# Second weight staged whole in the doubled filter's idle space, loads in one queue by need, four wide scaling products on GpSimd

## The chip, the cores and the metric

One core of a Trainium2 chip runs the kernel. The metric is the device time of one execution in microseconds (us). Every run named here was fast (granted TensorE clock 0.990 to 1.0 over the whole span; the granted clock is the share of full speed that the chip allows TensorE). Profiles come from one execution each; the span in a profile is some 2 us shorter than the time of its run.

## The reference, cut to what matters

```python
X = np.fft.rfft(x, axis=1)                 # x: (8, 3008, 256)
Y = X * (filt_r + 1j * filt_i)[None]       # a filter for each frequency and channel
x = np.fft.irfft(Y, n=3008, axis=1).reshape(24064, 256)
h = x @ w_in                               # 256 -> 2048
out = (h * sigmoid(beta * h)) @ w_out      # 2048 -> 256, float32
```

The kernel does each transform as two stages of small matmuls with a transposition between them (3008 = 47 x 64). Batch 0 is transposed on chip. From batch 1 on the transposition goes through DRAM: the first stage's result `a` is written to a scratch tensor `d` (the trace writes this "d<-a") and read back turned ("a<-d"). The feed-forward part runs all the while, and the transform of the next batch is slipped between its matmuls. An eviction is the copy of a matmul's result out of its accumulator into a tile.

## The kernel before: the parts that matter

The filter lives in two tiles. `fri` holds the real and the imaginary half; batch 0 uses it, so it is loaded first. `frr` holds the real half twice; only batch 1 and later need it, so for the first 46 us nothing is in it. The second weight must be scaled by 1/beta on its way to bf16. In the code `gp` and `nc.gpsimd` are GpSimd, `nc.sync` is SyncE, `nc.scalar` ScalarE; `place` slips work into the feed-forward loop.

```python
fri = consts.tile([P, NK, D], F32, ...)       # NK = 24 frequency groups, 3 MB
frr = consts.tile([P, NK, D], F32, ...)       # 3 MB, idle until batch 1
FG = ((0, KG), (KG, KG), (2 * KG, 2 * KG))    # parts of 6, 6 and 12 groups

def load_wout(f0, n):                         # a staging tile from a pool of two
    ws = ostp.tile([P, n, D], F32, name="ws", tag="ost")
    nc.sync.dma_start(ws[:], moe_w_out[f0 * P : (f0 + n) * P, :].rearrange(...))
    return ws

def scale_wout(ws, f0, n, eng):               # 4 calls x 4 products of 128x256
    for i in range(n):
        eng.tensor_scalar_mul(wout_sb[:, f0 + i, :], ws[:, i, :], rbeta_sb[:, f0 + i : f0 + i + 1])
# ... (first stage of batch 0, tables, loads of the first weight and of x1) ...
ws = [load_wout(i * WG, WG) for i in range(2)]
# ... (batch 0: products with fri, back transform) ...
for i in range(4):
    if i >= 2:
        ws.append(load_wout(i * WG, WG))      # waits for a staging tile, in SyncE's queue
    scale_wout(ws[i], i * WG, WG, gp)
for k0, n in FG:                              # the doubled filter: first part on SyncE, rest on GpSimd
    for at in (0, M):
        for go in load_filter(frr, filt_r, at, k0, n, gp if k0 else nc.sync):
            go()
# ... (feed-forward loop; slipped into it for batch 1:)
def s1(b, i, on_act):                         # first stage, then a write to DRAM
    ...
    if jj + 2 == JG:
        nc.sync.dma_start(s["d1r"][:, g * JG : (g + 1) * JG, :], s["a1"][:])      # d<-a, four per batch
def a2_read(b):                               # read back turned: a<-d, waits for all four writes
    for h in range(NG):
        nc.sync.dma_start(t[:], s["d1c"][:, h * KG : (h + 1) * KG, :])
```

In the trace of before, SyncE's transfers leave in program order: the third and fourth weight load wait 26.7 us in all for their staging tiles, and the filter's loads behind them leave only then, the first one at 46.27 us, right after the fourth weight load at 45.85.

Of the kernel before, what the change touches and what calls it, by code (L numbers as in the profile page):

```python
# [9 lines left out]
P = 128  # L10

ACT = mybir.ActivationFunctionType
ALU = mybir.AluOpType
F32 = mybir.dt.float32
BF16 = mybir.dt.bfloat16
# [9 lines left out]
M = 64  # L25
H = M // 2
NK = 24
J = 32
KG = 6
NG = NK // KG  # L30
JG = 8
# [5 lines left out]
def kernel(  # L37
# [10 lines left out]
    nc = tc.nc  # L48

    B, S, D = x.shape  # L50
    NF = filt_r.shape[0]
    DIN, FF = moe_w_in.shape
# [4 lines left out]
    NFB = FF // P  # L57
    NP = 2 * N1
# [7 lines left out]
    dpool = ctx.enter_context(tc.tile_pool(name="dram_scratch", bufs=2, space=bass.MemoryType.DRAM))  # L66

    def pool(name, bufs, **kw):
        return ctx.enter_context(tc.tile_pool(name=name, bufs=bufs, **kw))
# [3 lines left out]
    xpool = pool("xpool", 1)  # L73
# [6 lines left out]
    ostp = pool("ostp", 2)  # L80
# [5 lines left out]
    fri = consts.tile([P, NK, D], F32, name="fri", tag="fri")  # L86
    frr = consts.tile([P, NK, D], F32, name="frr", tag="frr")
# [9 lines left out]
    rbeta_sb = consts.tile([P, NFB], F32, name="rbeta_sb", tag="rbeta_sb")  # L97
    win_sb = wpool.tile([P, NDC, FF], BF16, name="win_sb", tag="win_sb")
    wout_sb = wpool.tile([P, NFB, D], BF16, name="wout_sb", tag="wout_sb")
# [3 lines left out]
    def evac(dst, src, on_act, scale=None):  # L103
        if on_act:
            nc.scalar.activation(dst, src, ACT.Copy, scale=1.0 if scale is None else scale)  # L105
        elif scale is None:
            nc.vector.tensor_copy(dst, src)  # L107
        else:
            nc.vector.tensor_scalar_mul(dst, src, scale)  # L109

    def load_x(b, parts):
        t = xpool.tile([NP, J, D], BF16, name="xg", tag="xg")
        xv = x[b].rearrange("(p j) d -> p j d", j=J)
        for p0, p1, j0, j1 in parts:
            nc.gpsimd.dma_start(t[p0:p1, j0:j1, :], xv[p0:p1, j0:j1, :])  # L115
        return t
# [3 lines left out]
    X_HALVES = [(0, 80, 0, J // 2), (80, NP, 0, J // 2), (0, 80, J // 2, J), (80, NP, J // 2, J)]  # L120
# [3 lines left out]
    def load_filter(f_sb, filt, at, k0, n, eng):  # L124
        lo = AP(filt.tensor, filt.offset + k0 * D, [[N1 * D, H], [1, n * D]])
        hi = AP(filt.tensor, filt.offset + (N1 - k0) * D, [[N1 * D, H], [-D, n], [1, D]])
        return [
            lambda: eng.dma_start(
                f_sb[at : at + H, k0 : k0 + n, :].rearrange("p k d -> p (k d)"), lo
            ),  # L130
            lambda: eng.dma_start(f_sb[at + H : at + M, k0 : k0 + n, :], hi),
        ]

    def load_wout(f0, n):
        ws = ostp.tile([P, n, D], F32, name="ws", tag="ost")
        nc.sync.dma_start(
            ws[:], moe_w_out[f0 * P : (f0 + n) * P, :].rearrange("(fb fp) j -> fp fb j", fp=P)
        )
        return ws

    def scale_wout(ws, f0, n, eng):
        for i in range(n):
            eng.tensor_scalar_mul(
                wout_sb[:, f0 + i, :], ws[:, i, :], rbeta_sb[:, f0 + i : f0 + i + 1]
            )


    sp = ctx.enter_context(ExitStack())
# [26 lines left out]
    def warm(n, cols=512):  # L175
        for _ in range(n):
            nc.tensor.matmul(pw[0][:, :cols], lhsT=wz[:, :P], rhs=wz[:, :cols], start=True, stop=True)
# [12 lines left out]
    gp = nc.gpsimd  # L190
# [6 lines left out]
    FG = ((0, KG), (KG, KG), (2 * KG, 2 * KG))  # L197
# [67 lines left out]
    def t2_part(h, part):  # L265
        u, r = us[h], rs[h]
        ks_ = slice(h * NH, (h + 1) * NH)
        if part == 0:
            nc.scalar.activation(t2[:, ks_, 2, :], u[:], ACT.Sin, scale=TWO_PI)
        elif part == 1:  # L270
            nc.scalar.activation(r[:], u[:], ACT.Abs)
        else:
            for cols, sgn, b in ((slice(0, H), -1.0, hp), (slice(H, M), 1.0, hm)):
                nc.scalar.activation(
                    t2[:, ks_, 1, cols], r[:, :, cols], ACT.Sin, scale=sgn * TWO_PI, bias=b[:]
                )

    def t2_more(h, eng):
        ks_ = slice(h * NH, (h + 1) * NH)
        eng.tensor_scalar_mul(t2[:, ks_, 4, :], t2[:, ks_, 1, :], -1.0)  # L280
        eng.tensor_copy(t2[:, ks_, 3, :], t2[:, ks_, 2, :])
        eng.tensor_copy(t2[:, ks_, 0, :], t2[:, ks_, 1, :])
# [10 lines left out]
    angles(0, nc.vector)  # L293
    angles(1, gp)

    for go in load_filter(fri, filt_i, M, *FG[2], gp):
        go()

    id_f = setup.tile([NFB, NFB], F32, name="id_f", tag="id_f")
    gp.tensor_copy(id_f[:], ident[:NFB, :NFB])  # L300
    tiny = setup.tile([NFB, P], F32, name="tiny", tag="tiny")
# [8 lines left out]
    held = setup.tile([P, 1], F32, name="held", tag="held")  # L310
    for p0 in (H, M + H):
        gp.tensor_copy(held[p0 : p0 + H], fri[p0 : p0 + H, 2 * KG - 1, :1])
    WI = 2
    for h in range(WI):
        fs = slice(h * FF // WI, (h + 1) * FF // WI)
        gp.dma_start(win_sb[:, :, fs], moe_w_in[:, fs].rearrange("(dc p) f -> p dc f", p=P))
    mark2 = dpool.tile([1, 2 * D], F32, name="mark2", tag="mark2")
    for c, p0 in enumerate((M - 1, P - 1)):
        nc.sync.dma_start(mark2[:, c * D : (c + 1) * D], fri[p0 : p0 + 1, 2 * KG - 1, :])
    WG = NFB // 4  # L320
    ws = [load_wout(i * WG, WG) for i in range(2)]


    a_t = ypool.tile([P, NDC, NK, J, 4], BF16, name="a_t", tag="y")

    def first1(i, on_act):
        for dc in range(NDC):
            if dc:
                ps = opsum.tile([P, 4, P], F32, name="psa", tag="acc")
            else:  # L330
                ps = fpsum.tile([P, 4, P], F32, name="psa", tag="f")
            for e in range(4):
                nc.tensor.matmul(
                    ps[:, e, :KP],
                    lhsT=x_cur[:, 4 * i + e, dc * P : (dc + 1) * P],
                    rhs=t1b[:],
                    start=True,
                    stop=True,
                )
            evac(  # L340
                a_t[:, dc, :, 4 * i : 4 * i + 4, :].rearrange("p k j a -> p j k a"),
                ps[:, :, :KP].rearrange("p j (k a) -> p j k a", a=4),
                on_act[dc],
            )
# [6 lines left out]
    warm(2)  # L351
    for part in (1, 2):
        t2_part(0, part)
    for i in range(3, 5):
        first1(i, (False, False))
        warm(2)
# [3 lines left out]
    first1(6, (True, True))  # L360
    warm(2)
    first1(7, (False, True))

    xs = {}
    if B > 1:
        xs[1] = load_x(1, X_HALVES)



    def table3(i, part, on_act):  # L370
        pt = opsum.tile([P, KG, P], BF16, name="pt", tag="acc")
        for e in range(KG):
            nc.tensor.transpose(
                pt[:, e, :],
                t2[:, KG * i + e, part : part + 2, :].rearrange("p c k -> p (c k)"),
                ident[:],
            )
        dst = t3 if part else t3b
        if i == 0:
            if part:  # L380
                evac(dst[:, 0, :], pt[:, 0, :], on_act, 0.5)
            else:
                nc.vector.tensor_scalar_mul(dst[:, 0, :], pt[:, 0, :], keep[:])
            evac(dst[:, 1:KG, :], pt[:, 1:KG, :], on_act)
        else:
            evac(dst[:, KG * i : KG * i + KG, :], pt[:], on_act)
# [76 lines left out]
    for i in range(NK // 2 + FLAG):  # L463
        if i < NK // 2:
            product(i)
        if i % 3 < 2 and i // 3 < 3:
            turn_a(2 + 2 * (i // 3) + i % 3, True)
        if i < 3:
            t2_part(1, i)
        if i % 3 > 0 and i // 3 < 3:  # L470
            table3(1 + i // 3, 4 - 2 * (i % 3), i % 3 == 1)
        if i == 3:
            t2_more(1, nc.vector)

            bps = hpsum.tile([P, NFB], F32, name="bps", tag="hps")
            nc.tensor.transpose(bps[:], bt[:], id_f[:])
            nc.vector.tensor_copy(beta_sb[:], bps[:])
            nc.vector.reciprocal(rbeta_sb[:], beta_sb[:])
        if i == 9:
            table4()  # L480
        if i >= FLAG:
            inverse3(i - FLAG)

    for i in range(4):
        if i >= 2:
            ws.append(load_wout(i * WG, WG))
        scale_wout(ws[i], i * WG, WG, gp)
    for k0, n in FG:
        for at in (0, M):
            for go in load_filter(frr, filt_r, at, k0, n, gp if k0 else nc.sync):  # L490
                go()

    ys = {}
# [218 lines left out]
    if B > 1:  # L712
        at = place(1, 11, u1(1, True), per=2)
        place(at + 1, at + 1, [lambda: a2_read(1)], per=9)
        at = place(22, 54, u23(1), per=2)
# [3 lines left out]
    if B > 2:  # L719
        place(36, 36, ux(2), per=9)  # L720
        at = place(50, 66, u1(2, True), per=3)
# [40 lines left out]
    for s in range(len(steps) + LAG):  # L762
        if s < len(steps):
            i, fb = steps[s]
# [4 lines left out]
            while pos < t0 + tn:  # L769
                b, n0 = divmod(pos, S)  # L770
# [18 lines left out]
        if s >= LAG:  # L789
            i, fb = steps[s - LAG]  # L790
# [18 lines left out]
            if fb == NFB - 1:  # L809
                ost = ostp.tile([P, 4, D], F32, name="ost", tag="ost")  # L810
                for h in range((nch + 1) // 2):
                    n = min(2, nch - 2 * h)
# [38 lines left out]
```

## Time and profile before

Before the change the median was 799.36 us (798.99 to 801.47, four runs).

| Reading | Value | View |
|---|---|---|
| TensorE busy | 772.4 of 797.2 us | page, busy line |
| TensorE waits for the read-back of batch 1 | 4.6 us, ends 71.2 us | waits, timeline |
| TensorE waits for an eviction whose buffer a d<-a write holds | 1.8 us, near 53 us | waits |
| last d<-a write, issue to landing | 8.6 us | chain |
| DMA share at 40 to 45 and 45 to 50 us | 0.42, 0.62 | table of stretches |

The page's busy line (us, share of the span, instructions):

```profile
PE 772.4 (97%) x6001; PEld 547.9 (69%) x6097; DVE 393.1 (49%) x642; ACT 597.2 (75%) x919; POOL 153.9 (19%) x161
```

TensorE's list of waits from 45 to 80 us (line, what it waited for: us in total, times, longest):

```profile
PE ps L611 <- DMA a<-d: 4.6, 1, 4.6
PE ps L512 <- ACT a L105: 1.8, 1, 1.8
```

SyncE's timeline (start us, us from the start of the first to the end of the last, queue, what, count). L136 is the fourth load of the second weight; L128 is the first of four loads of the doubled filter; L594 are the four d<-a writes; L601 is the read-back:

```profile
45.85 0.37 SPq L136 DMA_DIRECT2D ws<-in_moe_w_out_dram  x1
46.27 0.49 SPq L128 DMA_DIRECT2D frr<-in_filt_r_dram  x1
...
48.27 8.65 SPq L594 DMA_DIRECT2D d<-a  x4
65.40 1.77 SPq L601 DMA_DIRECT2D a<-d  x4
```

GpSimd's timeline: the last four scaling products, then the first of its eight loads of the doubled filter:

```profile
50.25 3.62 POOL L143 TENSOR_SCALAR wout_sb<-ws,rbeta_sb 128x256 bf16<-128x256 f32 x4 [0.84 <-DMA ws<-in_moe_w_out_dram]
53.82 0.56 POOL L128 DMA_DIRECT2D frr<-in_filt_r_dram  x1
```

The chain of waits from 44 to 72 us (start, us, what):

```profile
48.27 6.20 DMA d<-a
...
56.62 8.63 DMA d<-a
65.40 5.72 DMA a<-d
```

The table of stretches (the stretch, its length in us; then for TensorE, its weight loads, VectorE, ScalarE and GpSimd busy us and instruction count; then granted clock, DMA share, GB/s):

```profile
40.00:45.00 5.00, 4.95 (x40) 3.30 (x40) 3.69 (x6) 3.75 (x7) 2.80 (x4) 1.00 0.42 124
45.00:50.00 5.00, 5.00 (x37) 3.25 (x36) 2.55 (x4) 4.47 (x9) 4.41 (x5) 1.00 0.62 163
...
65.00:70.00 5.00, 1.57 (x11) 0.88 (x9) 0.42 (x1) 1.83 (x3) 0.00 (x0) 1.00 0.99 229
70.00:75.00 5.00, 3.61 (x20) 2.41 (x21) 2.62 (x4) 0.69 (x1) 1.03 (x1) 0.66 0.72 263
```

Read together: the fourth weight load leaves SyncE at 45.85 us, because it had to wait for a staging tile. The filter's first loads and the d<-a writes stand behind it. The last write is issued at 56.6 us and takes 8.63 us, the read-back another 5.72. TensorE has nothing to do from 66.6 to 71.2 us, and afterwards it gets a clock of 0.66 on average from 70 to 75 us. All the rest of the program is about 99% TensorE work (99.0 to 99.3 us in each 100 us from 200 to 700 us), so a microsecond that these waits lose is hardly made up later.

### The profile page before, as it was taken

What the parts mean: (1) busy time and instruction counts of PE and PEld (TensorE: products, weight loads), DVE (VectorE), ACT (ScalarE), POOL (GpSimd) and SP (SyncE); (2) the same over time, 40 slices, a digit from 0 to 9 for tenths busy, and PEclk for the clock granted to TensorE, in tenths of its full rate; (3) what the DMA queues carried; (4) which work ended last, traced back from release to release, by engine and by line L of the source; (5) the groups of instructions that cost most, each with busy time, mean ns of one, the idle gap of its engine ahead of it and who ended that gap; (6) DMA issues with size and microseconds to landing.
All of it is one profiled execution on the core that took longest, in us unless ns stands there. A gap on an engine that the chain in (4) does not pass through costs nothing.

```text
span 797.2 us, 15283 instructions
## 1 busy us (share of the span) xinstructions
PE 772.4 (97%) x6001; PEld 547.9 (69%) x6097; DVE 393.1 (49%) x642; ACT 597.2 (75%) x919; POOL 153.9 (19%) x161
## 2 busy tenths in 40 slices
PE   8897999999999999999999999999999999999997
PEld 5665767776677667776678766787667776776665
DVE  7834935674537556274644656357462770500100
ACT  6774887787678866788667886778767788677776
POOL 9371510340004300142001310023100340000000
PEclk9999999999999999999999999999999999999999
DMA  8987568324731168111780128602370114010101
GB/s 185 229 210 193 115 179 185 125 90 142 168 133 48 67 184 196 62 48 67 199 216 28 67 82 204 177 28 93 107 224 27 67 74 126 28 53 27 55 27 53
DMA packets 83733, 91.43 MB, mean 115 GB/s; under 512 B 3727, under 2 KB 74018, under 8 KB 82768
## 3 DMA queue, kind: packets, MB, share of 16 engines
q1 hardware_dynamic: 80446, 72.90, 29.4%
q0 software_dynamic: 2944, 17.30, 11.4%
q8 instruction: 47, 0.77, 0.4%
q10 hardware_dynamic: 272, 0.26, 0.1%
q14 instruction: 24, 0.20, 0.1%
HBM read 57.16 MB, written 46.66 MB: 130 GB/s over the span
## 4 chain that ended last, share of the span: by engine, by line
PE 87%; DMA 6%; DVE 3%; issue 2%; POOL 2%; ACT 0%; DVEq 0%; SPq 0%; ACTq 0%; POOLq 0%
PE acc L801 40%; PE hps L773 36%; DMA d<-a 3%; PE ps L589 3%; PE ps L512 3%; PE ps L611 2%; PE ps L637 2%; DMA fri<-in_filt_i_dram 1%; DMA a<-d 1%; DVE ost L107 1%; POOL xg L115 0%; DVE qb_t L432 0%; POOL r L260 0%; DVE pb_t L432 0%; DVE p_t L622 0%
## 5 line engine op out<-in xcount | busy, mean ns | idle before, releaser
L782 ACT ACTIVATE gT<-hps,beta_sb 128x512 bf16<-128x512 f32 x752 | 516.4, 687 | 181.9 <-PE hps L773 148.4
L801 PE MATMUL acc<-wout_sb,gT 128*128 128x256 bf16 x3008 | 455.8, 273 | 3.7 <-ACT ost L105 0.2
L773 PE MATMUL hps<-y,win_sb 128*128 128x512 bf16 (+7 forms) x1634 | 427.6, 350 | 0.4 <-DVE y L109 0.3
L801 PEld LDWEIGHTS <-gT 128*128 128x128 bf16 x3008 | 285.8, 98 | 132.4 <-issue 4.0
L773 PEld LDWEIGHTS <-win_sb 128*128 128x128 bf16 x1728 | 164.9, 98 | 24.9 <-issue 0.7
L627 POOL TENSOR_TENSOR v_t<-p_t,q_t 128x512 bf16<-128x512 f32 x84 | 106.7, 1270 | 370.6 <-DVE q_t L626 361.9
L107 DVE COPY ost<-acc 128x512 f32<-128x512 f32 x87 | 56.1, 683 | 195.3 <-PE acc L801 189.1
L107 DVE CAST a<-ps 96x512 bf16<-96x512 f32 x96 | 65.8, 687 | 89.1 <-PE ps L589 84.1
L109 DVE TENSOR_SCALAR y<-ps 128x376 bf16<-128x376 f32 (+2 forms) x120 | 64.5, 541 | 61.2 <-PE ps L512 61.0
L622 DVE TENSOR_TENSOR p_t<-ps,frr 128x512 f32<-128x512 f32 x84 | 58.1, 691 | 38.3 <-PE ps L611 36.9
L626 DVE TENSOR_TENSOR q_t<-ps,fri 64x512 f32<-64x512 f32 x84 | 58.3, 694 | 1.2
L623 DVE SCALAR_TENSOR_TENSOR q_t<-ps,fri 64x512 f32<-64x512 f32 x84 | 57.5, 684 | 1.1
L512 PEld LDWEIGHTS <-zz 96*128 96x128 bf16 x512 | 35.5, 98 | 31.4 <-issue 2.7
L105 ACT ACTIVATE z<-ps 128x512 bf16<-128x512 f32 x84 | 49.5, 589 | 0.4
L589 PE MATMUL ps<-xg,t 94*96 94x512 bf16 x112 | 41.9, 381 | 0.6
L512 PE MATMUL ps<-t,zz 96*128 96x94 bf16 x448 | 36.7, 204 | 1.1
L611 PE MATMUL ps<-a,t 128*128 128x256 bf16 x168 | 32.3, 274 | 5.6 <-DMA a<-d 5.3
L115 POOL DMA_DIRECT2D xg<-in_x_dram x22 | 12.0, 554 | 116.4 <-PE acc L801 97.7
L637 PE MATMUL ps<-v_t,t 128*128 128x256 bf16 x168 | 32.1, 273 | 0.3 <-DVE q_t L626 0.3
L611 PEld LDWEIGHTS <-t 128*128 128x128 bf16 x168 | 15.9, 98 | 20.1 <-issue 5.6
L589 PEld LDWEIGHTS <-t 94*96 94x96 bf16 x112 | 13.8, 123 | 11.9
L637 PEld LDWEIGHTS <-t 128*128 128x128 bf16 x168 | 15.6, 98 | 7.8 <-DVE q_t L626 0.5
(119 smaller groups left out, 201.9 us busy)
## 6 DMA issues: line engine op xcount, KB each, us to landing
out_dram<-ost SPq DMA_DIRECT2D x40, 512.0 KB, 2.8
d<-a SPq DMA_DIRECT2D x28, 384.0 KB, 7.0
a<-d SPq DMA_DIRECT2D x28, 384.0 KB, 5.6
d<-z SPq DMA_DIRECT2D x28, 384.0 KB, 2.3
zz<-d SPq DMA_DIRECT2D x28, 384.0 KB, 5.4
xg<-in_x_dram POOLq DMA_DIRECT2D x6, 1280.0 KB, 10.3
out_dram<-ost SPq DMA_DIRECT2D x20, 128.0 KB, 2.3
ws<-in_moe_w_out_dram SPq DMA_DIRECT2D x4, 512.0 KB, 23.9
```

The costliest lines, as they stand in the source:

```text
L107: nc.vector.tensor_copy(dst, src)
L109: nc.vector.tensor_scalar_mul(dst, src, scale)
L512: nc.tensor.matmul(ps[:, e, :NP], lhsT=zz[:, jj + e, dc * P : (dc + 1) * P], rhs=tab[:], start=True, stop=True,)
L589: nc.tensor.matmul(ps[:KP], lhsT=t1[:], rhs=s["x"][:, 2 * i : 2 * i + 2, :], start=True, stop=True)
L611: nc.tensor.matmul(ps[:, e, :], lhsT=t2[:, k0 + e, 3:5, :].rearrange("p c k -> p (c k)"), rhs=s["a2"][g][:, kk + e, :], start=True, stop=True,
L622: nc.vector.tensor_tensor(p_t[:], ps[:], frr[:, ks_, :], ALU.mult)
L626: nc.vector.tensor_tensor(q_t[:M], ps[M:P], fri[M:P, ks_, :], ALU.mult)
L627: nc.gpsimd.tensor_tensor(v_t[:], p_t[:], q_t[:], ALU.add)
L637: nc.tensor.matmul(ps[:, e, :], lhsT=t3[:, k0 + e, :], rhs=v_t[:, e, :], start=True, stop=True)
L773: nc.tensor.matmul(hps[:, pos - t0 : pos - t0 + ln], lhsT=win_sb[:, dc, fb * P : (fb + 1) * P], rhs=ys[b][:, dc, n0 : n0 + ln], start=(dc ...
L782: nc.scalar.activation(gT[:, :tn], hps[:, :tn], ACT.Silu, scale=beta_sb[:, fb : fb + 1])
L801: nc.tensor.matmul(acc[tb // 2][:, tb % 2, :], lhsT=gT[:, tb * P : (tb + 1) * P], rhs=wout_sb[:, fb, :], start=(fb == 0 and tb % 2 == 0), ...
```

## The change

The intent is to get rid of the wait for a staging tile. The weight goes in one piece into 16 of the 24 groups of `frr`, which is idle then. All its loads stand in GpSimd's queue, interleaved with x1 in the order of need; SyncE loads the free third of `frr` after a marker that waits for x1. The 16 products become four with a broadcast operand. Two small moves come with it: the last imaginary part of `fri` is issued from ScalarE, earlier than it was from GpSimd, and one eviction of a table goes from VectorE to ScalarE. Not in the cut below: x1's loads move up in the program, and SyncE's old marker before the weight loads (`mark2`, which waited for the second filter part) is gone. The core of the diff:

```diff
-    def load_wout(f0, n):
-        ws = ostp.tile([P, n, D], F32, name="ws", tag="ost")
-        nc.sync.dma_start(ws[:], moe_w_out[...])
+    def staged(i):
+        return frr[:, NK - NFB + i * WG : NK - NFB + (i + 1) * WG, :]
+    def load_wout(i):
+        nc.gpsimd.dma_start(staged(i), moe_w_out[i * WG * P : (i + 1) * WG * P, :].rearrange(...))
-        for i in range(n):
-            eng.tensor_scalar_mul(wout_sb[:, f0 + i, :], ws[:, i, :], rbeta_sb[:, f0 + i : f0 + i + 1])
+        nc.gpsimd.tensor_tensor(wout_sb[:, fs, :], staged(i),
+            rbeta_sb[:, fs].unsqueeze(2).broadcast_to([P, WG, D]), ALU.mult)
...
-    for go in load_filter(fri, filt_i, M, *FG[2], gp):          # after GpSimd's angle table
-        go()
+    for go in load_filter(fri, filt_i, M, *FG[2], nc.scalar):   # after ScalarE's first tables
+        go()
...
+    load_win(0); load_win(1); load_wout(0)
+    xs[1] = load_x(1, X_HALVES[:2])
+    load_wout(1)
+    load_x(1, X_HALVES[2:], xs[1])
+    nc.sync.dma_start(mark3[:], xs[1][:1, J - 1, :])            # holds SyncE until x1 is there
+    load_wout(2); load_wout(3)
...
-            table3(1 + i // 3, 4 - 2 * (i % 3), i % 3 == 1)
+            table3(1 + i // 3, 4 - 2 * (i % 3), i % 3 == 1 or i == 8)
...
-    for k0, n in FG:
+    for k0 in range(0, NK, JG):                                 # thirds of 8 groups
         for at in (0, M):
-            for go in load_filter(frr, filt_r, at, k0, n, gp if k0 else nc.sync):
+            for go in load_filter(frr, filt_r, at, k0, JG, gp if k0 else nc.sync):
                 go()
```

More of the change, by code (lines that the diff above doesn't have):

```diff
@@ L109, in evac, with load_x @@
             nc.vector.tensor_scalar_mul(dst, src, scale)
-    def load_x(b, parts):
-        t = xpool.tile([NP, J, D], BF16, name="xg", tag="xg")
+    def load_x(b, parts, t=None):
+        if t is None:
+            t = xpool.tile([NP, J, D], BF16, name="xg", tag="xg")
         xv = x[b].rearrange("(p j) d -> p j d", j=J)
@@ L132, in load_filter, with scale_wout @@
         ]
-    def load_wout(f0, n):
-        ws = ostp.tile([P, n, D], F32, name="ws", tag="ost")
-        nc.sync.dma_start(
-            ws[:], moe_w_out[f0 * P : (f0 + n) * P, :].rearrange("(fb fp) j -> fp fb j", fp=P)
-        )
-        return ws
-    def scale_wout(ws, f0, n, eng):
-        for i in range(n):
-            eng.tensor_scalar_mul(
-                wout_sb[:, f0 + i, :], ws[:, i, :], rbeta_sb[:, f0 + i : f0 + i + 1]
-            )
+    WG = NFB // 4
+    def staged(i):
+        return frr[:, NK - NFB + i * WG : NK - NFB + (i + 1) * WG, :]
+    def load_wout(i):
+        nc.gpsimd.dma_start(
+            staged(i),
+            moe_w_out[i * WG * P : (i + 1) * WG * P, :].rearrange("(fb fp) j -> fp fb j", fp=P),
+        )
+    def scale_wout(i):
+        fs = slice(i * WG, (i + 1) * WG)
+        nc.gpsimd.tensor_tensor(
+            wout_sb[:, fs, :],
+            staged(i),
+            rbeta_sb[:, fs].unsqueeze(2).broadcast_to([P, WG, D]),
+            ALU.mult,
+        )
     sp = ctx.enter_context(ExitStack())
@@ L312, with load_win @@
         gp.tensor_copy(held[p0 : p0 + H], fri[p0 : p0 + H, 2 * KG - 1, :1])
-    WI = 2
-    for h in range(WI):
-        fs = slice(h * FF // WI, (h + 1) * FF // WI)
+    def load_win(h):
+        fs = slice(h * FF // 2, (h + 1) * FF // 2)
         gp.dma_start(win_sb[:, :, fs], moe_w_in[:, fs].rearrange("(dc p) f -> p dc f", p=P))
-    mark2 = dpool.tile([1, 2 * D], F32, name="mark2", tag="mark2")
-    for c, p0 in enumerate((M - 1, P - 1)):
-        nc.sync.dma_start(mark2[:, c * D : (c + 1) * D], fri[p0 : p0 + 1, 2 * KG - 1, :])
-    WG = NFB // 4
-    ws = [load_wout(i * WG, WG) for i in range(2)]
+    load_win(0)
+    load_win(1)
+    load_wout(0)
+    xs = {}
+    if B > 1:
+        xs[1] = load_x(1, X_HALVES[:2])
+    load_wout(1)
+    if B > 1:
+        load_x(1, X_HALVES[2:], xs[1])
+        mark3 = dpool.tile([1, D], BF16, name="mark3", tag="mark3")
+        nc.sync.dma_start(mark3[:], xs[1][:1, J - 1, :])
+    load_wout(2)
+    load_wout(3)
     a_t = ypool.tile([P, NDC, NK, J, 4], BF16, name="a_t", tag="y")
@@ L362 @@
     first1(7, (False, True))
-    xs = {}
-    if B > 1:
-        xs[1] = load_x(1, X_HALVES)
     def table3(i, part, on_act):
@@ L484 @@
     for i in range(4):
-        if i >= 2:
-            ws.append(load_wout(i * WG, WG))
-        scale_wout(ws[i], i * WG, WG, gp)
-    for k0, n in FG:
+        scale_wout(i)
+    for k0 in range(0, NK, JG):
         for at in (0, M):
-            for go in load_filter(frr, filt_r, at, k0, n, gp if k0 else nc.sync):
+            for go in load_filter(frr, filt_r, at, k0, JG, gp if k0 else nc.sync):
                 go()
```

## The prediction

A gain of about 4.5 us off 799.35 gives 794.8. 250 to 270 GB/s for saturated DMA are an estimate from the table of stretches of before, where stretches with a share of 1.0 or more moved 191 to 282 GB/s (276, 282 and 261 from 50 to 65 us).

> **What bounds the kernel now.** TensorE: in the busy line of the profile it works 772.4 of 797.2 us (97%), and from 145 us on about 99% of every stretch in the table of stretches. The change touches only the first 75 us, so only TensorE's idle time there can be won. The list of its waits has two pieces that matter here:
> - 4.6 us at 66.6 us, for the read-back of batch 1's transposed first stage ("a<-d"). After it the granted clock is 0.66 from 70 to 75 us, and slow matmuls (four output matmuls in 0.85 us, not 0.44) cost about 1.3 us more. [...]
> - 1.8 us at 53.4 us, for an eviction that waited for the first "d<-a" write to free a buffer.
>
> Both come from SyncE's DMA queue. The third and fourth loads of the second weight (ws) wait there for a staging buffer; the fourth goes out at 46 us. Four filter loads follow, so the first d<-a issue comes at 48.3 us and the last at 56.6; that lands at 65.3, and its read-back gives data at 71.2 us. Meanwhile DMA's share is 0.42 at 40 to 45 us and 0.62 at 45 to 50, against 1.0 to 1.1 around it.
>
> **What the change does.**
> 1. All weight loads queue with x1 without waiting. The 40 to 50 us hole (about 1.1 MB below the saturated 250 to 270 GB/s, worth about 4 us) fills. SyncE's marker holds it until x1 has landed, at 42 to 43 us: the bytes up to there are the same and DMA is full from 5 to 40 us. First d<-a issue: about 45 us. The 1.8 us wait goes.
> 2. The scaling on GpSimd, 16 x 0.92 = 14.8 us, becomes four products of 128x1024. From v_t (1.27 us for 512) and u (1.46 us for 768) I estimate 2.0 to 2.5 us each. Off the critical path; it only sets when the filter's later two thirds load, from 50 to 53 us instead of 53.8.
> 3. The imaginary filter's last part goes out from ScalarE at about 12 us, not from GpSimd at 16.3. VectorE waited 1.2 us for it before the seventh product (27.7 us). But it now competes with the first part, and its two issues occupy ScalarE: I credit 0.3 us.
> 4. One table eviction (0.55 us) leaves VectorE, which is back to back from 27.7 to 35.4 us, for ScalarE: 0.4 us.
>
> **How much is critical.** The matmuls after the read-back start when the DMA chain ends. TensorE arrives about 2.5 us earlier (64 us). GpSimd's filter loads still compete with the last d<-a writes, so the read-back comes at about 67 us. A wait of about 3 us remains, with part of the slow clock. Gain about 4.5 us of 799.35, nearly all kept, since TensorE is saturated afterwards.
>
> **Predicted: 794.8 us, range 791 to 798.** Faster by over 2%: 0.01; within 2%: 0.98; slower: 0.01.
>
> **What would show it.** DMA share near 1 from 40 to 50 us; first d<-a issue near 45 us; no TensorE wait near 53 us; a wait for a<-d of 2 to 4 us ending at 66 to 68 us; four products of 2.0 to 2.5 us; VectorE's last filter product ending about 34.7 us.
>
> **What would make it wrong.** If d<-a loses to weight and filter loads queued at once, the read-back comes no earlier: 798 or more. If it runs ahead of the filter, both waits and the slow clock vanish: about 791. If the first filter part lands late, the first stage shifts by 1 to 2 us.

## The result, and the profile after

The changed kernel took 794.04 us (793.28 to 795.42, four runs), a ratio of 0.993 to before with a 95% interval of 0.9908 to 0.9952. A ratio is the mean time of one kernel's fast runs over that of the other's in the same rounds, so it is not quite the ratio of the medians. Repeated later as a control it gave 0.9952 (0.9931 to 0.9973). The gain is 0.5 to 0.7%, or 3.6 to 5.3 us by the medians: under 2%, but clear of noise.

The busy line after; 96 more matmuls are on record than before, which is a gap in the record of before (the count of weight loads is equal):

```profile
PE 776.2 (98%) x6097; PEld 547.4 (69%) x6097; DVE 393.2 (50%) x641; ACT 597.9 (76%) x920; POOL 149.3 (19%) x151
```

TensorE's list of waits from 45 to 80 us has one wait for DMA left, and the one near 53 us is gone:

```profile
PE ps L621 <- DMA a<-d: 2.1, 1, 2.1
```

SyncE's timeline: the marker, the first filter load, the four d<-a writes, the read-back:

```profile
40.91 0.23 SPq L333 DMA_DIRECT2D mark<-xg  x1
41.18 0.31 SPq L129 DMA_DIRECT2D frr<-in_filt_r_dram  x1
...
43.94 11.09 SPq L604 DMA_DIRECT2D d<-a  x4
62.77 1.78 SPq L611 DMA_DIRECT2D a<-d  x4
```

GpSimd's timeline: the last scaling product (1.89 us, one of four), then the first of the eight filter loads, 6 us earlier than before:

```profile
46.01 1.89 POOL L149 TENSOR_TENSOR wout_sb<-frr,rbeta_sb 128x1024 bf16<-128x1024 f32 x1 [0.84 <-DMA frr<-in_moe_w_out_dram]
47.85 0.58 POOL L129 DMA_DIRECT2D frr<-in_filt_r_dram  x1
```

The chain of waits, and the table of stretches for the same four stretches as before:

```profile
54.73 7.91 DMA d<-a
62.77 3.53 DMA a<-d
```

```profile
40.00:45.00 5.00, 4.91 (x41) 3.33 (x40) 3.85 (x6) 3.97 (x8) 1.73 (x1) 1.00 1.06 275
45.00:50.00 5.00, 5.00 (x37) 3.26 (x35) 2.25 (x4) 4.20 (x8) 4.16 (x6) 1.00 1.08 264
...
65.00:70.00 5.00, 3.66 (x31) 2.71 (x31) 3.15 (x5) 1.59 (x4) 1.06 (x1) 1.00 0.96 324
70.00:75.00 5.00, 4.69 (x41) 3.24 (x39) 4.84 (x8) 3.74 (x6) 2.13 (x3) 1.00 0.16 55
```

The profiled spans are 797.2 and 791.4 us, 5.8 us apart, and the two traces say where that went:

| Step | Before | After | Gained so far |
|---|---|---|---|
| first feed-forward matmul | 39.52 us | 38.97 us | 0.55 us |
| TensorE has done all before the read-back | 66.57 us | 64.24 us | 2.3 us |
| first matmul on the read-back | 71.17 us | 66.34 us | 4.8 us |
| end of the span | 797.2 us | 791.4 us | 5.8 us |

The clock gives the rest: it was 0.66 from 70 to 75 us before, and it is 1.00 in all of these stretches after. Both traces have all 752 evictions of the hidden layer (`gT`), so the lead can be followed one by one: 2.3 us up to the last one before the read-back, 6.3 us once the slow clock is over (75.03 us before is 68.73 after), which makes about 1.5 us for the clock. After 75 us 0.5 us of it is given back, about as much is won again near 140 us (the waits for the next read-back are 0.66 us before, 0.17 after), and from there the lead stays at 6.3 us to the last eviction. Another 0.5 us is lost after that one.

One thing got worse. VectorE's timeline shows a wait that was not there before, ahead of its fourth product with the filter (the bracket tells the idle time and its releaser):

```profile
21.90 0.69 DVE L444 TENSOR_TENSOR pb_t<-ps,fri 128x512 bf16<-128x512 f32 x1 [0.86 <-DMA fri<-in_filt_i_dram]
```

The part that now goes out earlier from ScalarE seems to slow the second filter part, which this product needs. In exchange the wait of 1.2 us ahead of the seventh product, which needs the part that was moved, is gone. VectorE's timeline before:

```profile
27.67 0.69 DVE L432 TENSOR_TENSOR pb_t<-ps,fri 128x512 bf16<-128x512 f32 x1 [1.22 <-PE ps2q L423]
```

(The profile of before puts that wait down to TensorE, but the seventh product's own matmuls had ended at 25.8 and 26.1 us, 1.6 us or more before it began; that it was the load fits its going away with the load's move.)

The exchange is not the rule. Of the eight profiles below and above with the move as it is in the change, only two have a wait ahead of the fourth product, the changed kernel and filter_late (0.86 and 0.94 us). Early_parts_only, narrow_scale and late_narrow have neither wait: their products take 17.2 us from the first start to the last end, against 18.3 before and 18.0 in the changed kernel. In these three SyncE's own filter loads left at 7.9 to 8.1 us, in the two with the wait at 9.0 to 9.2 us, with ScalarE's at 10.5 to 10.7 us in all five. In the other three the products began 2 us or more later.

### The profile page after: what moved, and what is told of

Read it like the earlier page. It is cut to its first block, busy times and chain, and to the rows that moved or that the text cites. A ratio compares the mean times of both kernels' runs of the same rounds, so it can differ in the third digit from the quotient of the medians.

```text
span 791.4 us, 15358 instructions
## 1 busy us (share of the span) xinstructions
PE 776.2 (98%) x6097; PEld 547.4 (69%) x6097; DVE 393.2 (50%) x641; ACT 597.9 (76%) x920; POOL 149.3 (19%) x151
## 3 DMA queue, kind: packets, MB, share of 16 engines
q1 hardware_dynamic: 78460, 71.06, 28.9%
## 4 chain that ended last, share of the span: by engine, by line
PE 88%; DMA 6%; DVE 3%; issue 1%; ACT 1%; SPq 0%; POOL 0%; DVEq 0%; POOLq 0%; ACTq 0%
PE acc L811 39%; PE hps L783 38%; PE ps L599 3%; DMA d<-a 2%; PE ps L522 2%; PE ps L621 2%; PE ps L647 2%; DMA fri<-in_filt_i_dram 1%; DVE ost L107 1%; DMA a<-d 1%; DMA xg<-in_x_dram 1%; DVE q_t L636 0%; ACT a L105 0%; DVE q_t L633 0%; DVE p_t L632 0%
## 5 line engine op out<-in xcount | busy, mean ns | idle before, releaser
L783 PE MATMUL hps<-y,win_sb 128*128 128x512 bf16 (+7 forms) x1728 | 447.7, 351 | 0.3 <-DVE y L109 0.3
## 6 DMA issues: line engine op xcount, KB each, us to landing
xg<-in_x_dram POOLq DMA_DIRECT2D x6, 1280.0 KB, 10.5
```

The costliest lines, as they stand in the source:

```text
L783: nc.tensor.matmul(hps[:, pos - t0 : pos - t0 + ln], lhsT=win_sb[:, dc, fb * P : (fb + 1) * P], rhs=ys[b][:, dc, n0 : n0 + ln], start=(dc ...
```

## The experiments

Three theories were to be told apart.

- Q: the gain is SyncE's queue. The d<-a writes leave and land earlier, so the read-back does. In its stricter form, Q with contention, what decides is how many bytes of the doubled filter move beside the last d<-a write.
- E: the gain is the shorter first stage (the two small moves), carried to the end.
- H, which the prediction leaned on: the gain is the hole in DMA use from 40 to 50 us, now filled.

All outputs are right. Each group of four ran on one chip and shares its runs of before.

### Group 1: which part of the change gains

**early_parts_only**: the kernel before with the two small moves alone.

```diff
-    for go in load_filter(fri, filt_i, M, *FG[2], gp): go()
+    for go in load_filter(fri, filt_i, M, *FG[2], nc.scalar): go()   # placed as in the change
-            table3(..., i % 3 == 1)
+            table3(..., i % 3 == 1 or i == 8)
```

> The kernel before with only the two early moves: the filter's last part issued from ScalarE, and one table eviction on ScalarE. Theory Q (the gain is SyncE's queue: earlier d<-a writes and read-back): SyncE is still held by the weight loads to about 46 us, so the read-back's data still comes at about 71 us and the time stays within 0.8 us of before (798.5 to 800). Rival E (the early moves give a shorter first stage that is carried to the end): the last filter product ends about 0.6 us earlier, the first hidden matmul comes at 39.0 instead of 39.5, and the time falls by 0.6 to 1.5 us.

It took 799.37 us, ratio 0.9995 (0.9978 to 1.0013). In its profile the first feed-forward matmul comes at 37.94 us, 1.6 us earlier than before, and the first matmul on the read-back at 70.20 us, only 1.0 us earlier: TensorE waits 2.3 us near 53 us and 4.7 us for the read-back. E as the explanation of 5 us falls. The interval doesn't exclude a gain of the size that E names, but the profile shows why little of it arrives: the next waits take it back.

**staging_only**: the changed kernel with both small moves undone (the diff above, reversed).

> The changed kernel with both early moves undone (the filter's last part from GpSimd again, the table eviction on VectorE again); staging, one queue and wide products stay. Theory Q: first d<-a issue near 44 us, no TensorE wait near 53 us, read-back data at 66 to 67 us, time 794 to 795.2. Rival E: at least 1.5 us slower than the changed kernel, 795.5 or more.

It took 797.12 us (793.26 to 798.5), ratio 0.9960 (0.9941 to 0.9980). That is slower than Q's figure and fits E's number, so taken by itself it would have been a point for E. But the interval overlaps those of both measurements of the changed kernel, and the marker, which shows when x1 is there, came at 44.20 us here, against 40.91 and, in the control, 43.98 us in the unedited changed kernel: the executions differ by that much without any edit. What can be said is that staging alone gives most of the gain and the small moves alone next to none. In this profile the hole is filled (DMA share 0.91 and 0.97 from 40 to 50 us), and yet TensorE waits 3.3 us for the read-back, whose first matmul comes at 69.10 us, not at 66 to 67. That was the first sign against H. Q's other sign was missed too: the wait near 53 us is not gone but 1.3 us, for the first d<-a write left at 46.3 us, not near 44. So staging helps this wait only as far as it lets that write leave early.

**narrow_scale**: the changed kernel with 16 narrow products.

```diff
-        nc.gpsimd.tensor_tensor(wout_sb[:, fs, :], staged(i), rbeta broadcast, ALU.mult)
+        for e in range(WG):
+            fb = i * WG + e
+            nc.gpsimd.tensor_scalar_mul(wout_sb[:, fb, :], staged(i)[:, e, :], rbeta_sb[:, fb : fb + 1])
```

> The changed kernel with the scaling as 16 products of 128x256 with a per-partition scalar instead of four of 128x1024. The products take 14.8 us instead of 7.6, so the last one ends near 51 us instead of 48 and the filter's later two thirds are issued about 3 us later. If those loads share DMA with the last d<-a write on its critical way (theory Q with contention): d<-a lands 1 to 2 us later, read-back data at 67.5 to 69 us, time up by 1 to 2.5 us over the changed kernel. Rival (the scaling is off the path and only frees GpSimd): same time as the changed kernel within 0.5 us.

It took 796.01 us, ratio 0.9947 (0.9931 to 0.9963): between the changed kernel's two measurements and not resolved by time. GpSimd's timeline shows the last eight products and the first filter load, 2.6 us later than after the change:

```profile
43.33 7.22 POOL L151 TENSOR_SCALAR wout_sb<-frr,rbeta_sb 128x256 bf16<-128x256 f32 x8 [0.56 <-DMA frr<-in_moe_w_out_dram]
50.49 0.59 POOL L129 DMA_DIRECT2D frr<-in_filt_r_dram  x1
```

The chain of waits shows what that does to the last d<-a write and to the read-back:

```profile
53.62 10.64 DMA d<-a
64.41 3.35 DMA a<-d
```

The write was issued 1.1 us earlier than in the changed kernel, but took 10.64 us instead of 7.91. TensorE waits 4.2 us, and the clock falls to 0.83 from 65 to 75 us. This is what contention expects of the profile: nothing reads the scaled weight late, only the filter loads moved.

**no_act_load**: the changed kernel with the filter part issued from GpSimd again.

```diff
-    for go in load_filter(fri, filt_i, M, *FG[2], nc.scalar): go()
+    for go in load_filter(fri, filt_i, M, *FG[2], gp): go()          # placed as before
```

> The changed kernel with only the filter's last imaginary part issued from GpSimd again, at about 16 us. Expected: the 0.9 us wait of VectorE before the fourth product (its filter part landing at 21.8 us) is gone, a wait of about 1.2 us before the seventh product (as in the kernel before) is back, the last product ends at 34.5 to 35.2 us (34.9 in the changed kernel), and the time is within 0.5 us of the changed kernel: the move shifted a wait from one product to another. Rival: the move gained the 1.2 us, so undoing it costs about 1 us.

It took 796.26 us, ratio 0.9958 (0.9938 to 0.9978), inconclusive. In this profile the first input arrived so late that the first products came 3 us late, and neither wait could show. Other profiles show one half: without the move the seventh product waits (1.22 us before, 1.28 in staging_only, 1.56 in before_filter_late), with it never. The other half, the wait ahead of the fourth product, came with the move in only two profiles of eight. What the move is worth in time stays unresolved.

### Group 2: order, and the last write

**after_again**: the changed kernel, unedited.

> The changed kernel, unedited, as the control for the other runs of this group: its ratio to before should again be 0.993 within 0.002. The read-back's data should come at 66 to 67.5 us in its profile and TensorE's wait for it should be 2 to 3 us; how far both move between profiles of one program says how much one profile can tell.

It took 795.90 us, ratio 0.9952 (0.9931 to 0.9973), by a hair outside what was expected. The read-back's first matmul came at 69.24 us, later than expected, with a wait of 1.9 us, just under the expected 2 to 3: the whole first stage was late in this execution. The wait is the steadier reading, the moment is not.

**no_marker**: the changed kernel without SyncE's marker.

```diff
-        nc.sync.dma_start(mark3[:], xs[1][:1, J - 1, :])
```

> The changed kernel without SyncE's marker behind x1, so that the first third of the doubled filter is issued at about 16 us and shares DMA with the first weight and x1. If all that counts is total bytes: the same time as the changed kernel within 0.7 us, d<-a issues at the same times. If the order of landing counts: 1 MB more ahead of x1 puts x1 about 4 us later (an estimate, 1 MB at 250 GB/s), the first stage of batch 1 waits for it at 40 us, and the time is 1 to 3 us above the changed kernel.

It took 798.22 us, ratio 0.9989 (0.9963 to 1.0015): nearly the whole gain is gone, so order counts and not the sum of the bytes. The size was as expected, the way was not. The first stage of batch 1 hardly waits for x1 (0.3 us). Instead the 1 MB that slipped ahead seems to delay the weight (the last scaling product ends at 52.6 us, after the change at 47.9) and hence the filter loads, which GpSimd issues from 52.5 us instead of 47.9. The last d<-a write then takes 10.8 us, and TensorE's list of waits shows this:

```profile
PE ps L619 <- DMA a<-d: 4.9, 1, 4.9
```

The clock after it is 0.50 from 70 to 76 us, the longest slow stretch of all runs.

**filter_late**: the changed kernel; the later two thirds of the doubled filter stand in SyncE's queue behind the read-back.

```diff
-            for go in load_filter(frr, filt_r, at, k0, JG, gp if k0 else nc.sync): ...
+            for go in load_filter(frr, filt_r, at, 0, JG, nc.sync): ...       # first third as it was
         place(at + 1, at + 1, [lambda: a2_read(1)], per=9)
+        place(at + 1, at + 1, [the loads of thirds two and three, on nc.sync], per=9)
```

> The changed kernel, with the later two thirds of the doubled filter issued from SyncE behind the read-back, not from GpSimd right after the scaling. Theory Q with contention: the last d<-a write, issued near 54.7 us, now has DMA almost to itself and lands in 3 to 5 us (7.9 in the changed kernel), the read-back's data comes at 60 to 62 us, before TensorE gets there at about 64 us; no wait over 0.5 us, no slow clock, and the time is 1.5 to 2.5 us below the changed kernel. Rival (the write is slow by itself[...]): it still lands 7 us or more after its issue, and the time is that of the changed kernel.

It took 792.89 us (791.59 to 793.77), ratio 0.9914 (0.9893 to 0.9935), against 0.9952 for the control on the same chip: 3.0 us less by the medians, where 1.5 to 2.5 were expected, and its slowest execution is faster than the control's fastest (793.88 us). As a control of the third group it gave 791.56 us, ratio 0.9898 (0.9872 to 0.9923). SyncE's list of waits, first in the changed kernel, then here: the wait of the read-back for the last write.

```profile
SPq L611 <- DMA d<-a: 7.6, 1, 7.6
```

```profile
SPq L615 <- DMA d<-a: 2.8, 1, 2.8
```

SyncE's timeline: the d<-a writes, the read-back, and the first of the filter loads behind it:

```profile
44.94 10.26 SPq L608 DMA_DIRECT2D d<-a  x4
58.09 1.78 SPq L615 DMA_DIRECT2D a<-d  x4
59.97 0.37 SPq L129 DMA_DIRECT2D frr<-in_filt_r_dram  x1
```

In the table of stretches TensorE is busy in full where the wait was; the filter's bytes have moved to 60 us and later:

```profile
55.00:60.00 5.00, 5.00 (x49) 3.78 (x48) 0.75 (x2) 4.00 (x7) 0.00 (x0) 1.00 0.44 108
60.00:65.00 5.00, 5.00 (x41) 3.54 (x39) 2.11 (x4) 3.99 (x7) 0.00 (x0) 1.00 1.03 345
65.00:70.00 5.00, 5.00 (x43) 3.55 (x41) 4.85 (x8) 3.10 (x6) 1.72 (x2) 1.00 1.08 216
```

There is no wait for this read-back in TensorE's list any more. The rival, that the write is slow by itself, falls: 2.8 us are enough. This version beats both kernels. One thing the edit doesn't separate: the loads move to another queue (from GpSimd's to SyncE's) as well as to a later time. No run has them late in GpSimd's queue; that it is the time is argued from the table at the end of this part, where all loads beside the write are GpSimd's and the write's time follows their bytes.

**filter_late_sp**: filter_late with the last imaginary filter part on SyncE, behind its own real half.

```diff
-    for go in load_filter(fri, filt_i, M, *FG[2], nc.scalar): go()
+    for go in load_filter(fri, filt_i, M, *FG[2], nc.sync): go()     # right after the real half
```

> As filter_late, with the last imaginary filter part issued from SyncE behind its own real half, so that it no longer runs beside the second part. Expected: neither VectorE's wait before the fourth product (0.9 us in the changed kernel) nor the one before the seventh (1.2 us before the change); the last product ends 0.5 to 1 us earlier than in the changed kernel, and since no read-back wait is left to swallow it, the time is 0.3 to 1 us below filter_late. Rival: the part lands after the seventh product needs it, and the time is that of filter_late or more.

It took 792.54 us, ratio 0.9913 (0.9890 to 0.9936): the same as filter_late. The fourth product does not wait, but the seventh, at 28.9 us, waits 0.65 us. The products began 2 us later than in the changed kernel, so the first half says little. The rival is closer. In this profile a wait of 1.5 us near 55 us is back: the first d<-a write left at 46.95 us.

### Group 3: is the staging needed at all?

**filter_late_again** is the control of this group (numbers above).

> filter_late once more, as the control of this group: 0.990 to 0.993 of before, no TensorE wait for the read-back over 0.5 us.

In its profile, too, TensorE does not wait for the read-back.

**before_filter_late**: the kernel before, with only the placing of the filter's later parts changed.

```diff
-            for go in load_filter(frr, filt_r, at, k0, n, gp if k0 else nc.sync): ...
+            for go in load_filter(frr, filt_r, at, *FG[0], nc.sync): ...
         place(at + 1, at + 1, [lambda: a2_read(1)], per=9)
+        place(at + 1, at + 1, [the loads of FG[1] and FG[2], on nc.sync], per=9)
```

> The kernel before, with nothing but the doubled filter's parts from the seventh frequency on issued from SyncE behind the read-back instead of from GpSimd. If the contention of these loads with the last d<-a write is what made the 4.6 us wait: that write, issued near 56.6 us, lands in about 3 us, the read-back's data comes at 63 us, the wait and the slow clock go, only the 1.8 us wait near 53 us stays, and the time is 5 to 6 us below before (793.5 to 795), as much as the whole change gives, without any staging. Rival (the gain needs the DMA hole at 40 to 50 us filled): the wait shrinks by less than 2 us and the time stays above 797.

It took 793.29 us (792.90 to 794.57), ratio 0.9922 (0.9899 to 0.9945), 6.9 us under before by the medians, a little more than expected. SyncE's timeline: the writes leave no earlier than before (48.57 against 48.27 us), and still the read-back goes out at 59.8 us, where before it was 65.4:

```profile
48.57 8.31 SPq L598 DMA_DIRECT2D d<-a  x4
59.79 1.77 SPq L605 DMA_DIRECT2D a<-d  x4
61.61 0.42 SPq L128 DMA_DIRECT2D frr<-in_filt_r_dram  x1
```

TensorE's list of waits keeps only the wait near 53 us, and the table of stretches shows the hole as wide open as before:

```profile
PE ps L516 <- ACT a L105: 2.0, 1, 2.0
```

```profile
40.00:45.00 5.00, 4.95 (x41) 3.38 (x41) 3.69 (x6) 3.91 (x7) 2.50 (x3) 1.00 0.33 98
45.00:50.00 5.00, 5.00 (x37) 3.26 (x35) 2.40 (x4) 4.47 (x9) 4.71 (x6) 1.00 0.55 158
...
55.00:60.00 5.00, 4.82 (x27) 2.82 (x27) 0.83 (x2) 2.93 (x6) 0.00 (x0) 0.66 0.53 150
```

The clock of 0.66 from 55 to 60 us was not expected: the wait of 2.0 us cost it here. The mean clocks say that this was not so each time: the two executions of this kernel at 794.6 us have 0.997 and 0.998, the four at 792.9 to 793.4 us 0.999 to 1.0.

H as what the gain needs falls with this run. The hole stays (0.33 and 0.55), nothing is staged, nothing is scaled otherwise, and the gain is as large as that of the whole change (the intervals overlap). What it doesn't show is that filling the hole does nothing in the changed kernel: there the weight lands earlier, and this is also what lets the filter loads start earlier.

**late_narrow**: filter_late with the 16 narrow products (the diff of narrow_scale on top of filter_late).

> filter_late with the 16 narrow products instead of the four wide ones. If the wide products only mattered by when they let the filter be loaded (the narrow ones alone cost the changed kernel about 1 us of read-back wait), they matter no more here: the time is that of filter_late within 0.7 us and no wait of TensorE for the second weight is seen. Rival (the products themselves hold something): 1 us or more slower.

It took 790.83 us (789.31 to 792.95), ratio 0.9889 (0.9863 to 0.9916), the lowest of all, but within the interval of filter_late (0.9898). TensorE waits for no weight. Without the filter loads behind them, the wide products are worth nothing that can be measured.

**late_act_later**: filter_late with ScalarE's two loads after the last evictions of the first stage.

```diff
     first1(7, (False, True))
+    for go in load_filter(fri, filt_i, M, *FG[2], nc.scalar): go()   # was after ScalarE's first tables
```

> filter_late with ScalarE's two loads of the last imaginary filter part issued some 3 us later, after the first stage's last evictions, so that they run less beside the second part. Expected: VectorE's wait before the fourth product (0.9 us in the changed kernel) shrinks below 0.4 us, no wait before the seventh, the last product ends about 0.5 us earlier after its first one; time 0 to 0.7 us below filter_late. Rival: the seventh product then waits, and nothing is gained.

It took 791.88 us, ratio 0.9906 (0.9880 to 0.9933), the same as filter_late. The profile has no wait ahead of the fourth product or of the seventh, and the last product ends at 34.43 us (34.85 in the changed kernel). That the edit took the wait away is not shown: in this profile SyncE's own loads left early (7.9 us), and late_narrow and narrow_scale, with ScalarE's loads where they were, have no such wait either. From the first product's start to the last one's end it is 17.8 us, 0.2 less than in the changed kernel, where 0.5 was expected, and 0.6 more than in late_narrow. The time resolves nothing.

### All last writes side by side

From each profile: when GpSimd issues its first load of the doubled filter, when the last d<-a write is issued, how far the loads were ahead of it, the piece "d<-a" in the chain of waits, that piece with the read-back's "a<-d" added, the bytes that GpSimd's queue (only filter loads by then) moved in this time by the view of DMA queues, and TensorE's wait for the read-back.

| Kernel | First filter load | Last write issued | Head start | Write took | Write and read-back | Filter loads beside them | TensorE waited |
|---|---|---|---|---|---|---|---|
| no_act_load | 47.4 us | 56.8 us | 9.4 us | 6.6 us | 9.9 us | 0.45 MB | 0.5 us |
| after_again | 49.6 us | 57.8 us | 8.2 us | 7.9 us | 11.2 us | 0.80 MB | 1.9 us |
| changed kernel | 47.9 us | 54.7 us | 6.9 us | 7.9 us | 11.4 us | 0.97 MB | 2.1 us |
| staging_only | 51.1 us | 55.8 us | 4.7 us | 9.8 us | 13.3 us | 1.61 MB | 3.3 us |
| no_marker | 52.5 us | 56.2 us | 3.7 us | 10.8 us | 14.3 us | 1.82 MB | 4.9 us |
| narrow_scale | 50.5 us | 53.6 us | 3.1 us | 10.6 us | 14.0 us | 1.79 MB | 4.2 us |
| kernel before | 53.8 us | 56.6 us | 2.8 us | 8.6 us | 14.4 us | 2.07 MB | 4.6 us |
| early_parts_only | 52.8 us | 55.5 us | 2.7 us | 11.3 us | 14.6 us | 2.06 MB | 4.7 us |
| filter_late, before_filter_late, late_narrow | behind the read-back | 54.9, 56.6, 53.5 us | none | about 3 us | not read | none beside the write | none |

The further the filter loads are ahead of the last write, the less of them is left to move beside it. In the write alone the kernel before breaks the order: 1.75 MB of filter move beside its write of 8.6 us. That its loads are cut differently (6 and 12 groups, not 8 and 8) can't be the reason, for early_parts_only has the same cut and takes 11.3 us. But 0.32 MB more of them move beside its read-back, which takes 5.7 us where the others take 3.3 to 3.5. Write and read-back together follow the bytes in all eight, to within 0.3 us: from 9.9 us with 0.45 MB to about 14.5 with 2.1 MB. This sum is what TensorE waits for. The "about 3 us" is the read-back's wait in SyncE's list (2.7 to 2.8 us) plus the issue of the write.

## Why the prediction was right

The forecast was 794.8 us (791 to 798); measured were 794.04 us and, in the control, 795.90 us. Point by point:

- *All weight loads queue without waiting, SyncE is free at 42 to 43 us, first d<-a at about 45 us.* Right: marker 40.9, first write 43.9 us (44.0 and 47.0 in the control). DMA's share from 40 to 50 us was 1.06 and 1.08, near 1 as forecast (0.79 and 1.02 in the control).
- *The wait near 53 us goes.* Right for the changed kernel and its control; with a little later first write it is back (1.3 us in staging_only).
- *TensorE arrives at about 64 us, the read-back comes at about 67 us, a wait of about 3 us remains.* Right: 64.24, 66.34 and 2.1 us (67.3, 69.2 and 1.9 in the control).
- *Filling the hole is worth about 4 us.* The number of the sum came out, its reason did not; that much was luck. Before_filter_late leaves the hole open and gains as much; staging_only fills it and still waits 3.3 us. What had to be said is that the filter's 2 MB must not move beside the last write. The text named this contention, but only as what limits the gain, when it was what the wait was made of. The change eases it in passing: its filter loads start 6 us earlier, so that more of them are through when the last write comes (in single profiles, narrow_scale puts 2.6 us of these down to the wide products, which leaves 3.3 for the earlier weight).
- *Part of the slow clock remains.* Wrong: after a wait of 2.1 us the clock stayed at 1.00, worth about 1.5 us by the lead. That was luck as well: a wait as long, 2.0 us, cost the clock in before_filter_late (more in the last section).
- *Four products of 2.0 to 2.5 us.* A little too long: 1.89 us. *Off the critical path, it only sets when the filter loads.* Right, and this was the more important sentence: narrow_scale and late_narrow show that this is all they do.
- *The moved part competes with the first part; 0.3 us credited.* It was the second part that lost (a wait of 0.86 us ahead of the fourth product). The last product ended at 34.85 us, 0.6 us earlier than before; forecast was 34.7 us. Counted from the first product's start it was 0.35 us, half of the 0.7 us credited to both moves.
- *If d<-a runs ahead of the filter, both waits and the slow clock vanish: about 791.* No forecast of the change, but filter_late is the nearest case, for the last write: 792.9 and 791.6 us.

## What to carry to other kernels

Before making a transfer start earlier, look at what moves beside the one transfer that the busiest engine waits for. Here placing loads that nobody needs yet behind that transfer gave as much, in a few lines, as a restaged weight, a new queue order and wider products together (ratios 0.9922 and 0.993). In early_parts_only a gain of 1.6 us was 1.0 us behind two waits, and the ratio came to 0.9995: follow the chain to its last link, and change that link first.

## What the traces show of the clock, the queues and GpSimd

- The clock: by the clock record in the trace of before it was 0.50 for 3.41 us, from 70.8 to 74.2 us. The tables of stretches of early_parts_only, staging_only and before_filter_late show 0.50 too, for about 3.4 us by their means; that of narrow_scale shows 0.58 and 0.57 from 68 to 72 us, which would come to the same, and that of no_marker 0.50 for about 6.8 us. TensorE's waits before or into these slow stretches were 4.6 us (before), 4.7, 3.3, 2.0, 4.2 and 4.9 us, in this order. Waits of 2.3 us (early_parts_only, near 53 us), 2.1 us (changed kernel), 1.9 us (after_again) and 1.8 us (before, near 53 us) cost nothing: the clock stayed at 1.00. So a wait of 2.0 us cost the clock where waits of 2.1 and 2.3 us did not. The length of a wait alone does not decide it here; what else does was not shown.
- A write beside other loads: a d<-a write of 384 KB took about 3 us with no filter load beside it (filter_late) and 6.6 to 11.3 us beside filter loads from another queue. Write and read-back together took 9.9 us beside 0.45 MB of these and about 14.5 us beside 2.1 MB.
- GpSimd: the product of 128x1024 with a broadcast operand took 1.89 us, 1.85 ns per element of a row; the product of 128x256 with a per-partition scalar took 924 ns, 3.6 ns per element. The sizes differ there, but at one size, 128x768 in float32, adding and subtracting a constant on one input took 2.81 us, and single operations on two inputs 1.46 and 1.81 us. In these profiles the form with two inputs was the faster one.
- Scatter: executions of one program differed by 2 to 6 us of 800 within a group of runs, which hid every step below 1.5 us.
